# Issuing 32 stores of an inverse transform from ScalarE's DMA queue instead of SyncE's

## The chip, the core and the metric

The kernel runs on one core of a Trainium2 chip. Five engines work side by side, each with its own queue of instructions: TensorE (PE in the profile; its weight loads are shown apart as PEld), VectorE (DVE), ScalarE (ACT), GpSimd (POOL) and SyncE (SP). They wait for each other through semaphores. A DMA is issued by an instruction in the queue of SP, ACT or POOL; the bytes are moved by 16 DMA engines that all queues share, and a counter tells when they have landed. The metric is the device time of one execution in microseconds, lower is better.

## What is computed

The result mixes two branches of the same input `x` (2048 positions, 512 channels) by a gate per position. One branch is a long convolution along the positions, whose taps `K` come from a state-space model and which the reference does by FFT; the other is a dense layer pair with GELU.

```python
x = A_u
g = _sigmoid((x * gate_w).sum(-1, keepdims=True))
P = jnp.exp(logdA[:, :, None] * l[None, None, :])
K = jnp.einsum("dn,dnl,dn->dl", Cc, P, dB).real
Yf = Uf * Kf[None, :, :, :]          # spectra of u and K, padded to 2 L
y = irfft2(Yf, s=(1, L2))[:, :, 0, :L] + u * Dskip
h = _gelu(jnp.einsum("bsd,df->bsf", x, w1) + b1)
b = jnp.einsum("bsf,fd->bsd", h, w2) + b2
return g * a + (1 - g) * b           # a is y
```

## The kernel before

The program has two parts. `front` (to about 420 us of the profile) computes the dense branch, the taps and the first stage of the transforms of taps and signal. A planner with due times sets the order of its instructions; it leaves the first-stage results in DRAM (`tu_d` for the signal, `tk_d` for the taps) and the dense branch's rows in the output. The change does not touch it.

`conv` (L1091 to L1289) does the rest, in an order that is written out by hand. The transform of length 2048 is split into 32 x 64, and `conv` holds the 32 second-stage transforms, two per loop step, so 16 steps `s`. The tiles are 128 partitions x 512 channels of fp32 (256 KB). In step `s`:

- `product(s)` multiplies the spectra of signal and taps on DVE (six operations, L1151 to L1156).
- `signal(s + 1)` runs eight matmuls on PE into the banks `p2u` (L1129), from the tiles `us`, which lie in `den`, `attic` and `loft`.
- `matrices(s // 2 + 1)` in even steps makes the second set of factors `f` from the constants `cc`, by two ACT instructions (L1117, L1118).
- `taps(s + 2)` runs eight matmuls into `p2k` (L1129), four with weights from `cc` and four with weights from `f`, and ACT copies the two banks to `k` (L1137).
- `inverse(s)` runs eight matmuls into the two banks `pa` (L1168).
- `turn(s)` copies each `pa` to one of six buffers `sa` by ACT (L1174) and stores `sa` to the DRAM tensor `t4_d` (L1176; the profile calls it `t_d`). After every eighth row, a group of `t4_d` is complete and is read back in another layout, into `den` and `t3` (profile: `t`), by POOL's queue for the first three groups and by ACT's for the last (L1188).
- In steps 7 to 12 `dense` loads rows of the dense branch from the output by SP's queue (L1202).

At each step's start SP issues the loads that come next: `tk` (L1110), `cc` (L1102), `tu_d` (L1241). So SP's queue holds loads and stores in the order of the loop, and a store that waits for ACT's copy holds back the loads behind it.

After the loop PE does what was left of the dense products (`rest`, L1213 to L1215), and the last transform `pb` over `den` and `t3` (L1273, 64 matmuls); DVE or ACT and POOL apply the gate and add, and the rows go out (L1287, L1289).

Every DMA from SP or ACT also takes one of eight completion counters, DMAHW0 to DMAHW7, in turn, whichever of the two queues issues it. A DMA that takes a counter again first waits until the DMA that carried it last has landed.

Of the kernel before, what the change touches and what calls it, by code (L numbers as in the profile page):

```python
# [275 lines left out]
def gated_mix(  # L276
# [18 lines left out]
    nc = tc.nc  # L295
# [5 lines left out]
    t4_d = dr.tile([4, 2, GROUP, 2, 32, D], F32, name="t4_d")  # L301
# [789 lines left out]
    def conv(pool, ps, late, attic, loft, den):  # L1091


        sas = [pool.tile([P, D], F32, name=f"sa{k}", bufs=1) for k in range(6)]
# [75 lines left out]
        def turn(s):  # L1170

            for n in (2 * s, 2 * s + 1):
                sa = sas[n % 6]
                nc.scalar.copy(sa, pas.pop(n))  # L1174
                g, k = divmod(n, GROUP)
                nc.sync.dma_start(t4_d[g, :, k].rearrange("e c q d -> (c q) e d"), sa)  # L1176
                if k < GROUP - 1:
                    continue
                rows = t4_d[g].rearrange("e k c q d -> (e k c) q d")

                for h in (0, 4, 8, 16, 24) if g == 3 else (0, 8, 16, 24):
                    if h == 24 and g < 2:
                        held.append((t3[g:P:4, 16:24], rows[:, 24:32]))
                        continue
                    on = nc.gpsimd if n < 31 else nc.scalar
                    e = h + (4 if g == 3 and h < 8 else 8)
                    to = t3[g:P:4, h - 8 : e - 8] if h > 7 else den[g:P:4, h:e]
                    on.dma_start(to, rows[:, h:e])  # L1188
# [41 lines left out]
        for s in range(16):  # L1230

            for n in range(2 * s + N_TK + (2 if s else 0), 2 * s + N_TK + 4):
                if n < 24:
                    fetch(n if n < 16 else n + 8)
            if s == 0:
                for n in range(16, 24):
                    fetch(n)
            if s in (2, 4, 6, 8):
                consts(s // 2 + 3)
            for n in range(2 * s + N_ROOM, min(2 * s + N_ROOM + 2, 32)) if s > 3 else ():  # L1240
                nc.sync.dma_start(us[n], tu_d[ko[n]])  # L1241
            product(s)
            if s + 1 < 16:
                signal(s + 1)
            if s + 2 < 16:
                if s % 2 == 0:
                    matrices(s // 2 + 1)
                taps(s + 2)
            if s == 9:
                for to, rows in held:  # L1250
                    nc.gpsimd.dma_start(to, rows)
            if s == 15:
                rest(N_REST)
            inverse(s)
            turn(s)
            if 7 <= s < 13:
                dense(HERE[s - 7], nc.sync)
# [4 lines left out]
        for s in range(4):  # L1262
            m, i = 7 - s // 2, s % 2
            z, g = mos[m][:, i], gate[:, 1, 2 * m + i : 2 * m + i + 1]
            nc.vector.scalar_tensor_tensor(z, accs[s], g, z, ALU.mult, ALU.add)

        for m in range(8):
# [9 lines left out]
            for i in range(2):  # L1277
                t = 2 * m + i
                z, g = mos[m][:, i], gate[:, 0, t : t + 1]
# [90 lines left out]
```

## Time and profile before

| | us |
|---|---|
| median of 3 runs | 530.65 |
| lowest and highest of them | 528.84, 531.64 |
| the profiled execution, its own time | 528.3 |
| its span, first to last instruction | 526.5 |
| PE busy in the span | 509.1 (97%) |
| ACT busy | 353.0 (67%) |
| DVE busy | 428.4 (81%) |
| granted TensorE clock, mean | 0.997 |

A row of the page's list of groups gives the line, the engine and operation, output and inputs by the program's names, the count, and then busy time and the mean of one in ns. A row of the timeline gives start and length in us, the same names, and in brackets how long the engine stood idle before it and what ended that. An engine with a q behind its name is its queue: issuing a DMA or waiting there is not counted as busy. "Landing" is the time from the issue of a DMA until its counter shows that all bytes have arrived. The chain of waits is followed back from the last instruction, at each step to what released it.

### The profile page before, as it was taken

What the parts mean: (1) busy time and instruction counts of PE and PEld (TensorE: products, weight loads), DVE (VectorE), ACT (ScalarE), POOL (GpSimd) and SP (SyncE); (2) the same over time, 40 slices, a digit from 0 to 9 for tenths busy, and PEclk for the clock granted to TensorE, in tenths of its full rate; (3) what the DMA queues carried; (4) which work ended last, traced back from release to release, by engine and by line L of the source; (5) the groups of instructions that cost most, each with busy time, mean ns of one, the idle gap of its engine ahead of it and who ended that gap; (6) DMA issues with size and microseconds to landing.
All of it is one profiled execution on the core that took longest, in us unless ns stands there. A gap on an engine that the chain in (4) does not pass through costs nothing.

```text
span 526.5 us, 12296 instructions
## 1 busy us (share of the span) xinstructions
PE 509.1 (97%) x4858; PEld 387.8 (74%) x4858; DVE 428.4 (81%) x808; ACT 353.0 (67%) x614; POOL 41.6 (8%) x80
## 2 busy tenths in 40 slices
PE   8887999999999999999999999999999999999995
PEld 7656789898889978976988998988988722222551
DVE  6898899999999968879999989999901188777543
ACT  4989946699875689986595998456534545565311
POOL 2000000000000000000012001202010100110123
PEclk9999999999999999999999999999999999999998
DMA  8999664152685434392879026625669899999978
GB/s 241 369 301 285 222 223 153 67 202 54 159 224 201 142 91 132 111 300 86 220 156 301 3 81 126 159 40 121 201 202 172 226 309 319 366 347 375 301 277 329
DMA packets 82517, 107.87 MB, mean 205 GB/s; under 512 B 39334, under 2 KB 43562, under 8 KB 81916
## 3 DMA queue, kind: packets, MB, share of 16 engines
q1 hardware_dynamic: 76476, 85.04, 50.8%
q0 software_dynamic: 5056, 18.65, 14.0%
q10 hardware_dynamic: 928, 3.41, 1.8%
q8 instruction: 38, 0.62, 0.5%
q14 instruction: 19, 0.16, 0.1%
HBM read 61.46 MB, written 45.62 MB: 203 GB/s over the span
## 4 chain that ended last, share of the span: by engine, by line
PE 75%; ACT 11%; DMA 8%; DVE 3%; issue 2%; SPq 1%; ACTq 0%; DVEq 0%
PE pk L693 10%; PE ph L915 8%; PE ph L917 8%; PE ph L916 8%; PE acc L965 8%; PE acc L967 7%; PE acc L966 7%; PE p2u L1129 6%; PE p2k L1129 5%; PE pa L1168 3%; PE pb L1273 3%; DMA tu_d<-attic 2%; PE ph L415 2%; ACT L932 2%; ACT ph L932 2%
## 5 line engine op out<-in xcount | busy, mean ns | idle before, releaser
L915 PE MATMUL ph<-xh,wh 128*128 128x256 f32 x448 | 128.1, 286 | 2.9 <-ACT attic L433 1.8
L917 PE MATMUL ph<-xh,wl 128*128 128x256 f32 x448 | 127.0, 284 | 0.5 <-DVE wl L794 0.4
L916 PE MATMUL ph<-xlo,wh 128*128 128x256 f32 x448 | 126.6, 283 | 0.0
L915 PEld LDWEIGHTS ph<-xh,wh 128*128 128x128 f32 x448 | 85.1, 190 | 11.9 <-issue 5.6
L916 PEld LDWEIGHTS ph<-xlo,wh 128*128 128x128 f32 x448 | 85.2, 190 | 2.0
L917 PEld LDWEIGHTS ph<-xh,wl 128*128 128x128 f32 x448 | 85.1, 190 | 1.2 <-DVE wl L794 1.2
L965 PE MATMUL acc<-wh,hh 128*128 128x512 f32 x206 | 82.9, 403 | 1.3 <-ACT hh L935 1.2
L967 PE MATMUL acc<-wh,hl 128*128 128x512 f32 x206 | 81.1, 394 | 0.4 <-DVE hl L945 0.4
L966 PE MATMUL acc<-wl,hh 128*128 128x512 f32 x206 | 80.9, 393 | 0.0
L932 ACT ACTIVATE ph<-ph,b1t 128x256 f32<-128x256 f32 x112 | 50.4, 450 | 43.3 <-PE ph L917 41.3
L945 DVE TENSOR_TENSOR hl<-ph,hh 128x512 fp32r<-128x512 f32 (+1 forms) x62 | 38.3, 618 | 31.9 <-ACT hh L935 31.6
L693 PE MATMUL pk<-y,den 128*32 128x64 f32 x2048 | 61.4, 290 | 0.0
L693 PEld LDWEIGHTS pk<-y,den 128*32 128x32 f32 x2048 | 57.2, 136 | 3.7 <-issue 1.4
L965 PEld LDWEIGHTS acc<-wh,hh 128*128 128x128 f32 x206 | 38.7, 188 | 15.9 <-issue 6.8
L967 PEld LDWEIGHTS acc<-wh,hl 128*128 128x128 f32 x206 | 38.7, 188 | 10.6 <-DVE hl L945 2.0
L655 DVE TENSOR_TENSOR y<-y,ea 128x64 f32<-128x64 f32 (+4 forms) x80 | 45.2, 566 | 0.2
L966 PEld LDWEIGHTS acc<-wl,hh 128*128 128x128 f32 x206 | 38.7, 188 | 6.5
L935 ACT CAST hh<-ph 128x512 fp32r<-128x512 f32 (+1 forms) x62 | 33.0, 533 | 8.7 <-PE acc L966 5.2
L500 DVE TENSOR_TENSOR loft<-den,zz 128x256 f32<-128x256 f32 (+2 forms) x48 | 37.2, 775 | 1.7 <-ACT den L626 1.3
L501 DVE TENSOR_TENSOR loft<-den,zz 128x256 f32<-128x256 f32 (+2 forms) x48 | 37.1, 773 | 0.0
L668 DVE TENSOR_TENSOR y<-y,loft 128x2048 f32<-128x2048 f32 x16 | 36.5, 2283 | 0.0
L1137 ACT COPY k<-p2k 128x512 f32<-128x512 f32 x32 | 18.8, 586 | 24.9 <-issue 13.1
(183 smaller groups left out, 885.2 us busy)
## 6 DMA issues: line engine op xcount, KB each, us to landing
tu_d<-attic SPq DMA_DIRECT2D x64, 128.0 KB, 3.6
tk_d<-sk SPq DMA_DIRECT2D x32, 256.0 KB, 4.7
t_d<-sa SPq DMA_DIRECT2D x32, 256.0 KB, 6.8
tk<-tk_d SPq DMA_DIRECT2D x24, 256.0 KB, 4.9
t<-t_d POOLq DMA_DIRECT2D x9, 512.0 KB, 8.3
attic<-in_xt_dram SPq DMA_DIRECT2D x16, 256.0 KB, 4.4
xh_d<-xh SPq DMA_DIRECT2D x8, 512.0 KB, 3.2
xl_d<-xlo SPq DMA_DIRECT2D x8, 512.0 KB, 4.9
```

The source lines that it names most:

```text
L500: vec(2 * m, lambda: vv.tensor_mul(t, a, br), due, [ka, *kb], [kt])
L655: nc.vector.tensor_mul(both(n, 64 - 3 * n, n), both(0, 64 - n, n), an)
L693: nc.tensor.matmul(pks[q][32 * j : 32 * j + 32, :, gg], x[:, r, :, ch], y[:, r, :, ch], start=(r == 0), stop=(r == 1), skip_group_check=True,)
L915: nc.tensor.matmul(p, h, xh[xk][:, d], start=(d == 0), stop=False)
L916: nc.tensor.matmul(p, h, xlo[xk][:, d], start=False, stop=False)
L917: nc.tensor.matmul(p, lo, xh[xk][:, d], start=False, stop=(d == 3))
L932: nc.scalar.activation(phs[q][:, n], phs[q][:, n], AF.Gelu_apprx_tanh, bias=b1t[:, f : f + 1])
L945: nc.vector.tensor_sub(lo, phs[q][:, 0:nf], hi.bitcast(F32))
L965: nc.tensor.matmul(a, h, wh[1][w], start=start, stop=False)
L966: nc.tensor.matmul(a, h, wl[1][w], start=False, stop=False)
L967: nc.tensor.matmul(a, l, wh[1][w], start=False, stop=(j == 3))
L1129: nc.tensor.matmul(out[64 * i : 64 * i + 64], w, x, start=True, stop=True)
```

## The change

`turn` now makes both copies of a step first and then issues both stores, from ACT's queue instead of SP's. Everything else is as before; the lines behind L1174 move down by one (L1176 is now L1177, L1188 is L1189, L1202 is L1203).

```diff
             for n in (2 * s, 2 * s + 1):
                 sa = sas[n % 6]
                 nc.scalar.copy(sa, pas.pop(n))
+            for n in (2 * s, 2 * s + 1):
                 g, k = divmod(n, GROUP)
-                nc.sync.dma_start(t4_d[g, :, k].rearrange("e c q d -> (c q) e d"), sa)
+                nc.scalar.dma_start(t4_d[g, :, k].rearrange("e c q d -> (c q) e d"), sas[n % 6])
                 if k < GROUP - 1:
                     continue
```

ACT's queue where step 1 ends and step 2 begins (`sa_4794` and `sa_4795` are the two buffers of step 1, `f_4967` the factors that `taps(4)` needs in step 2; the brackets name what an instruction waits for):

```order
 L1174 COPY sa_4794<-pa_4937 128x512 [waits PE_49]
 L1174 COPY sa_4795<-pa_4940 128x512 [waits PE_49]
+L1177 DMA t_d<-sa_4794 64x2x512 [waits DMAHW2_49,Activation_49]
+L1177 DMA t_d<-sa_4795 64x2x512 [waits DMAHW3_49,Activation_49]
 L1117 ACTIVATE f_4967<-cc_4814 64x256 [waits DMAHW0_49]
 L1118 COPY f_4967<-cc_4814 64x256
```

The two stores now stand between the copies of `pa` and the two instructions that make `f`. The second waits for the counter DMAHW3, which the second store of step 0 carried last.

ACT's queue in the change, from the stores of step 4 to the factors of step 6 (`sa_4794` and `sa_4795` are again the buffers of step 4, `sa_4796` and `sa_4797` those of step 5):

```order
L1177 DMA t_d<-sa_4794 64x2x512 [waits DMAHW2_49,Activation_49]
L1177 DMA t_d<-sa_4795 64x2x512 [waits DMAHW4_49,Activation_49]
L1137 COPY k_5099<-p2k_5096 128x512 [waits DVE_49,PE_49]
L1137 COPY k_5104<-p2k_5101 128x512 [waits PE_49]
L1174 COPY sa_4796<-pa_5106 128x512 [waits DMAHW6_49,PE_49]
L1174 COPY sa_4797<-pa_5109 128x512 [waits DMAHW7_49,PE_49]
L1177 DMA t_d<-sa_4796 64x2x512 [waits DMAHW0_49,Activation_49]
L1177 DMA t_d<-sa_4797 64x2x512 [waits DMAHW2_49,Activation_49]
L1117 ACTIVATE f_5137<-cc_4951 64x256 [waits DMAHW1_49]
L1118 COPY f_5137<-cc_4951 64x256
```

The first store of step 4 takes DMAHW2, and the second of step 5 is the next to take it, one step later.

SP's queue from step 6 on, as the difference:

```order
+L1242 DMA attic<-tu_d 128x512
+L1203 DMA attic<-out_dram 128x2x512
 L1102 DMA cc_5198<-in_c_dram 128x384
-L1176 DMA t_d<-sa_4796 64x2x512
-L1176 DMA t_d<-sa_4797 64x2x512
-L1202 DMA attic<-out_dram 128x2x512
-L1176 DMA t_d<-sa_4792 64x2x512
-L1176 DMA t_d<-sa_4793 64x2x512
-L1202 DMA attic<-out_dram 128x2x512
```

SP keeps the loads alone, and the loads of the dense rows no longer stand behind stores.

## The prediction, made before the changed kernel ran

> **What bounds the kernel now.** I read the page's chain first, then the window table of the last stage (the one the change touches), then the chain in order of time, then the timeline of one loop step.
>
> ```profile
> PE 75%; ACT 11%; DMA 8%; DVE 3%; issue 2%; SPq 1%; ACTq 0%; DVEq 0%
> ```
>
> ```profile
> 424.50:491.90 67.40, 67.40 (x355) 18.49 (x351) 54.76 (x90) 37.76 (x71) 6.20 (x12) 1.00 0.95 334
> 491.90:505.60 13.70, 13.70 (x62) 10.09 (x62) 4.17 (x7) 2.15 (x4) 0.00 (x0) 1.00 0.80 273
> 505.60:520.10 14.50, 13.96 (x65) 5.34 (x64) 7.59 (x11) 4.12 (x6) 7.38 (x6) 1.00 0.99 368
> 520.10:526.50 6.40, 0.00 (x0) 0.00 (x0) 0.67 (x1) 0.00 (x0) 0.23 (x1) 0.72 0.66 254
> ```
>
> The columns are stretch, sum, busy time of PE, PEld, DVE, ACT and POOL, granted clock, DMA share, GB/s. In the loop (first row) PE is busy all 67.40 us at clock 1.00; ACT is busy 37.76 of them and the DMA engines 0.95. So TensorE sets the loop's length, ACT has 44% to spare, and the DMA engines are nearly full. PE goes on without a gap to 505.6.
>
> ```profile
> 433.74 1.87 PE p2u L1129 x8
> 435.61 1.72 PE p2k L1129 x8
> 437.32 1.02 PE pa L1168 x8
> 438.34 1.87 PE p2u L1129 x8
> 496.51 6.42 DMA t_d<-sa
> 503.02 2.87 DMA den<-t_d
> 506.02 13.97 PE pb L1273 x64
> 520.02 0.75 DVE attic L1285
> ```
>
> A step lasts 438.34 - 433.74 = 4.60 us and is three PE pieces. SP's stores (L1176) appear on the chain only once: the last one lands 6.42 us after its issue at 496.51. Even there PE has the leftover dense products until 505.6, so what that landing costs is the gap up to 506.02, 0.42 us.
>
> **What the change can gain.** It cannot shorten the 67.40 us that are all PE. Two places are left. The first is the 0.42 us gap. The second is the tail after 520.1, which waits for output stores behind DMA engines that are 0.99 busy from 505.6 on. In the row before, 20% of 13.70 us = 2.7 us of DMA time is idle, because loads wait for the last t4_d stores; stores that land sooner could use at most that, so the tail is worth 0 to 2.7 us. Output stores are still released one pair at a time by PE's products and the last by DVE at 520.8. I take the gap in full and 0.4 us of the tail: **-0.8 us**, between 0 and -3.1.
>
> **What it costs: ACT's own queue.** This is an even step before:
>
> ```profile
> 433.80 1.07 ACT L1174 COPY sa<-pa 128x512 f32<-128x512 f32 x2 [0.37 <-PE pa L1168]
> 434.41 1.18 SPq L1176 DMA_DIRECT2D t_d<-sa  x2
> 434.90 0.41 ACT L1117 ACTIVATE f<-cc 64x256 f32<-64x256 f32 x1
> 435.32 0.40 ACT L1118 COPY f<-cc 64x256 f32<-64x256 f32 x1
> 435.87 0.14 PEld L1129 LDWEIGHTS p2k<-tk,f 128*64 128x64 f32 x2 [0.28 <-ACT f L1118]
> 436.30 1.03 PE L1129 MATMUL p2k<-tk,f 128*64 128x512 f32 x4
> 436.58 0.59 ACT L1137 COPY k<-p2k 128x512 f32<-128x512 f32 x1 [0.86 <-ACT f L1118]
> ```
>
> Right behind the two evictions sa stand the two copies that build f (L1117, L1118), and PE multiplies by f in the same step at 436.30. The stores now stand between them. The copies occur six times behind stores:
>
> ```profile
> L1117 ACT ACTIVATE f<-cc x6: 414/414/415, 434.9 to 480.9; 64x256 f32<-64x256 f32 x6
> L1176 SPq DMA_DIRECT2D t_d<-sa x32: 518/544/1326, 429.8 to 496.5; - x32
> 503.02 1.16 ACTq L1188 DMA_DIRECT2D den<-t_d  x2
> 504.28 1.84 ACTq L1188 DMA_DIRECT2D t<-t_d  x3
> ```
>
> An issue takes 0.544 us on SP (up to 1.326), and on ACT's queue 1.16 / 2 = 0.58 to 1.84 / 3 = 0.61 us. How late may f be? The start of the stage shows PE waiting for it:
>
> ```profile
> 419.72 0.40 ACT L1118 COPY f<-cc 64x256 f32<-64x256 f32 x1
> 420.17 1.08 PE L1129 MATMUL p2k<-tk,f 128*64 128x512 f32 x4 [0.80 <-ACT f L1118]
> L1137 ACTq EVENT_SEMAPHORE  x1: 2673/2673/2673, 433.9 to 433.9; - x1
> ```
>
> PE starts 0.05 us after f ends (420.12 to 420.17). In the step above f ends at 435.72 and is wanted by 436.30 - 0.05 = 436.25: a slack of 0.53 us. From below: the first store starts while the second eviction still runs, as SP's did (434.41, when the first eviction was done), the pair takes SP's 1.18 us to 435.59, f runs 435.62 to 436.44, PE starts at 436.49: 0.2 us late. From above: ACT issues only when both evictions are done (434.87) and takes 2 x 0.61 us, f runs 436.11 to 436.93, PE starts 0.7 us late; with issues as long as SP's slowest, nearly 1 us, f would run 436.90 to 437.72 and PE be 1.5 us late. The last row speaks for the lower end: ACT's queue stood at the wait of the k copy (L1137) at 433.9, 0.1 us after the first eviction began, with three instructions still to run; the queue goes ahead of its engine, so a store can be issued beside an eviction. Issues in a stage with a DMA share of 0.95 are sometimes long, though. I take 0.35 us a step: 6 x 0.35 = **+2.1 us**, between 1.2 and 6 (a mean of 1 us a step).
>
> The Trainium skill, Perfetto Trace Analysis, section on per-engine timelines, says that ACT's compute instructions are pushed into a wait queue and the sequencer goes on, while a DMA holds the sequencer until its descriptors are written. The trace agrees for the first half (the row at 433.9); by that rule alone the term would be 6 x 0.2 = 1.2 us and the sum below 0.9 us less.
>
> Odd steps have no f:
>
> ```profile
> 429.20 1.07 ACT L1174 COPY sa<-pa 128x512 f32<-128x512 f32 x2 [0.36 <-PE pa L1168]
> 431.98 0.59 ACT L1137 COPY k<-p2k 128x512 f32<-128x512 f32 x1 [1.71 <-issue]
> ```
>
> ACT idles 1.71 us between them and the pair of issues fits, so those cost nothing. If that cover were gone, k would be late, and it is read by DVE two steps on. SP is rid of 32 x 0.544 = 17.4 us of issuing that bounded nothing; its loads (tk, cc, the dense rows) come forward, and as PE had no gap, none was late.
>
> **Waits that ACT takes over.** The order shows each DMA waiting for one of eight counters (DMAHW0 to 7) used in turn: it may start only when the DMA that last carried its counter has landed. SP paid this before:
>
> ```profile
> SPq L1110 <- DMA t_d<-sa: 2.6, 2, 2.4
> 447.47 0.54 POOL L1188 DMA_DIRECT2D den<-t_d  x1 [33.50 <-DVE v L1155]
> 448.07 1.05 POOL L1188 DMA_DIRECT2D t<-t_d  x2
> 452.83 1.69 SPq L1176 DMA_DIRECT2D t_d<-sa  x2
> ```
>
> A tk load that reads nothing of t4_d waited up to 2.4 us for a store. Nobody felt it, since only loads stood behind. Now such a wait stands on ACT in front of f. In the order of the change the second store of step 1 waits for the second of step 0, 4.6 us older (DMAHW3), and the second of step 5 for the first of step 4 (DMAHW2). How long stores take to land, from issues of SP in three places:
>
> ```profile
> L1176 SPq DMA_DIRECT2D t_d<-sa x2: 552/562/572, 429.8 to 430.5; - x2
> DMA to landing us min/median/max: 6.8/6.8/6.8
> ...
> L1176 SPq DMA_DIRECT2D t_d<-sa x2: 530/542/553, 443.6 to 444.2; - x2
> DMA to landing us min/median/max: 2.4/2.4/2.4
> ...
> L1176 SPq DMA_DIRECT2D t_d<-sa x2: 530/554/579, 448.2 to 448.9; - x2
> DMA to landing us min/median/max: 8.7/8.7/8.7
> ```
>
> With 6.8 us the store of step 0 lands at 430.5 + 6.8 = 437.3 where step 1 wants to go on at 435.0: 2.3 us. With 8.7 us that of step 4 lands at 448.2 + 8.7 = 456.9, where step 5 wants to issue its second store 0.6 us after the 452.83 of its first: 3.5 us. Together 5.8 us from above. From below nothing: with 2.4 us both are in time. In a queue of its own a store no longer stands behind eight t loads (step 0), but at 448 POOL's three 512 KB loads take the engines whichever queue the store is in. I take nothing for step 1 and about half of 3.5 for step 5: **+1.8 us**.
>
> **Sum.** 2.1 + 1.8 - 0.8 = +3.1 us on a profiled execution of 528.3 us (span 526.5): 531.4. That execution is 2.3 us under the median of the runs shown, 530.65, on which the forecast is 530.65 + 3.1 = 533.8 us, 0.6% slower. I call a difference under 0.5% (2.65 us) no change, since that is about what a measurement of this kernel can tell; the three runs alone spread by 2.8 us.
>
> The Trainium skill, DMA: Bandwidth & Descriptors, section "Issuing engines are not separate DMA queues", says that issuing from several engines saves only the sequencer's issue time. Without the 0.4 us of tail that I granted to the separate queue the sum would be +3.5 us; no run here shows it yet.
>
> **Rivals.**
>
> *ACT issues only behind its own evictions, and slowly.* For it: issues of SP up to 1.326 us, DMA share 0.95. Against: the queue's place at 433.9. 6 x 1.0 + 1.8 - 0.8 = +7.0 us: 537.7.
>
> *Hidden after all.* The issues overlap the evictions, the stores land at 2.4 to 5 us in their own queue, and no counter is waited for: 1.2 + 0 - 1.5 (half of the 3.1 us at the end) = -0.3 us: 530.4, no change. For it: ACT's 44% of spare time, 0.53 us of slack. Against: the copies of f stand directly behind the stores, and the burst at 448.
>
> *Faster: the last stores.* One mechanism: today the last store needs 6.42 us because SP's queue is full ahead of it; alone in a queue it lands in 2.4 us, the loads for the final products come 4 us sooner, and the idle 2.7 us of DMA time before 505.6 is filled, so the output finds free engines. Price -0.42 - 2.7 = -3.1 us with the f copies costing nothing: 527.5. It decides only if f is late by less than 0.1 us a step. Against it: POOL's loads are in flight then too, and f has to end 0.53 us after where it ends now while 1.2 us are put ahead of it.
>
> The Trainium skill, Perfetto Trace Analysis, section DMA Optimizations, advises giving inputs to one issuing engine and outputs to another. By that rule this last rival would win.
>
> **How the numbers follow.** Forecast 0.50 (its own range 532 to 536), slow issue 0.22, hidden 0.23, faster 0.05. A quarter of the forecast's weight lies under +2.65 us. Slower: 0.50 x 0.75 + 0.22 = 0.6; within 0.5%: 0.125 + 0.23 = 0.35; faster 0.05. The range runs from 529.5 (hidden, less a run's spread) to 539 (slow issue with a little of the counters' upper bound).
>
> **What would show it.** f's first copy some 0.7 us later behind sa (1.8 instead of 1.1 us) in six steps; idle time of PE before p2k<-tk,f, released by ACT f, of about 0.35 us each; one longer gap around 453 to 456 where an ACT store waits for a landing; odd steps still 4.60 us long; PE's pb starting without the 0.42 us gap. I am wrong if even steps stay at 4.60 us (then f had more slack than I read), if odd steps stretch, or if PE waits for tk or attic loads.

## The result, and the profile after

With the stores on ScalarE's queue the kernel takes 532.81 us (median of 22 runs, 530.25 to 538.04), the kernel before, in the same measurement, 528.54 us (22 runs). The ratio is 1.0081 with a 95% interval of 1.0060 to 1.0102: 0.8% slower, 4.3 us by the medians, 3.2 to 5.4 us by the interval. The forecast was +3.1 us. The kernel before had a median 2.1 us lower here than in the three runs that the forecast was added to, so the difference, not the 533.8, is what the forecast has to be measured by. The profiled execution took 531.52 us, its span 529.7. Three executions in the measurements below, one each of three kernels, ran at a granted clock of 0.56 and took about 790 us; every median and ratio here leaves them out.

The chain of waits by engine, in the page of the changed kernel:

```profile
PE 73%; ACT 11%; DMA 7%; DVE 4%; issue 3%; SPq 1%; ACTq 1%; DVEq 0%
```

PE loses two points, and ACTq, the queue of ACT, has 1% where it had 0.

The window table of the changed kernel, cut at the same events as before: the loop, the leftover products, `pb`, the end.

```profile
424.50:496.55 72.05, 68.66 (x355) 17.92 (x351) 54.69 (x90) 37.53 (x71) 6.18 (x12) 1.00 0.93 325
496.55:510.20 13.65, 13.65 (x63) 10.11 (x63) 4.19 (x7) 2.15 (x4) 0.00 (x0) 1.00 0.81 282
510.20:524.25 14.05, 13.95 (x65) 4.51 (x64) 7.56 (x11) 4.12 (x6) 7.38 (x6) 1.00 0.87 326
524.25:529.70 5.45, 0.00 (x0) 0.00 (x0) 0.70 (x1) 0.00 (x0) 0.27 (x1) 0.91 0.67 251
```

The loop is 4.65 us longer for the same 355 matmuls at the same clock of 1.00, and TensorE, busy all of the stretch before, now idles 72.05 - 68.66 = 3.39 us of it. The other stretches are as long as before or shorter.

The chain in order of time shows what stands there instead. This is step 4 of the changed kernel, a step with nothing unusual in it (start, length, engine, output, line):

```profile
443.50 1.06 PE pa L1168 x8
...
445.06 0.60 ACT sa L1174
...
445.81 0.56 ACTq L1177
...
446.84 0.41 ACT f L1118
...
447.30 1.07 PE p2k L1129 x3
```

Before, a step was three PE pieces in a row. Now the chain leaves PE after `pa`, goes through ACT's second eviction (until 445.66), the issue of the second store (445.81 to 446.37), the copies of `f`, and comes back to PE at 447.30.

The timeline of ACT, for steps 2, 4, 6 and 8 of the changed kernel (L1174 are the two evictions, L1177 the two stores together; in brackets what ended the idle time):

```profile
433.76 1.07 ACT L1174 COPY sa<-pa 128x512 f32<-128x512 f32 x2 [0.42 <-PE pa L1168]
434.37 2.51 ACTq L1177 DMA_DIRECT2D t_d<-sa  x2
436.93 0.41 ACT L1117 ACTIVATE f<-cc 64x256 f32<-64x256 f32 x1 [2.10 <-DMA t_d<-sa]
...
444.57 1.07 ACT L1174 COPY sa<-pa 128x512 f32<-128x512 f32 x2 [0.42 <-PE pa L1168]
445.19 1.18 ACTq L1177 DMA_DIRECT2D t_d<-sa  x2
446.42 0.41 ACT L1117 ACTIVATE f<-cc 64x256 f32<-64x256 f32 x1 [0.77 <-ACT sa L1174]
...
454.67 2.01 ACTq L1177 DMA_DIRECT2D t_d<-sa  x2
456.73 0.41 ACT L1117 ACTIVATE f<-cc 64x256 f32<-64x256 f32 x1 [1.60 <-issue]
...
465.34 1.58 ACTq L1177 DMA_DIRECT2D t_d<-sa  x2
466.96 0.41 ACT L1117 ACTIVATE f<-cc 64x256 f32<-64x256 f32 x1 [1.42 <-DMA attic<-tu_d]
```

A pair of stores takes 1.18 us where nothing holds it (step 4), in the other three 2.51, 2.01 and 1.58. In steps 2 and 8 the second store waited for a DMA to land, in step 6 its issue alone was long.

How much each step lost can't be read from PE's idle time alone. From the timeline of PE I took the start of the first matmul into `pa` in every step and the distance to that of the step before; the "loop" is from step 0 to step 15. All odd steps up to 13 are 4.60 us in both kernels.

| us | loop | step 2 | 4 | 6 | 8 | 10 | 12 |
|---|---|---|---|---|---|---|---|
| before | 66.05 | 4.60 | 4.60 | 4.60 | 4.60 | 4.60 | 4.60 |
| changed | 70.73 | 6.21 | 4.88 | 5.71 | 5.63 | 4.99 | 4.91 |
| changed, profiled again | 71.74 | 7.88 | 4.88 | 5.00 | 5.63 | 4.90 | 5.02 |

The loop's 4.7 to 5.7 us account for the 4.3 us of the medians. In steps 2, 4 and 6 of the first profile a simple sum gives the loss: a step loses what `f` ends later behind the start of the evictions than it did before (1.92 us), less the slack of 0.53 us, plus 0.05 us because the first matmuls after a wait take 1.08 us in place of 1.03. For step 2: `f` starts at 436.93, its second copy ends at 437.76, 4.00 us behind 433.76; 4.00 - 1.92 - 0.53 + 0.05 = 1.60, measured 1.61. (In step 8 the evictions start late as well, held up by the stores of step 6.)

### The profile page after: what moved, and what is told of

Read it like the earlier page. It is cut to its first block, busy times and chain, and to the rows that moved or that the text cites. A ratio compares the mean times of both kernels' runs of the same rounds, so it can differ in the third digit from the quotient of the medians.

```text
span 529.7 us, 12267 instructions
## 1 busy us (share of the span) xinstructions
PE 512.7 (97%) x4858; PEld 389.3 (73%) x4858; DVE 428.5 (81%) x808; ACT 352.5 (67%) x614; POOL 41.6 (8%) x80
## 4 chain that ended last, share of the span: by engine, by line
PE 73%; ACT 11%; DMA 7%; DVE 4%; issue 3%; SPq 1%; ACTq 1%; DVEq 0%
PE pk L693 9%; PE ph L915 8%; PE ph L917 8%; PE ph L916 8%; PE acc L965 8%; PE acc L967 7%; PE acc L966 7%; PE p2k L1129 4%; PE p2u L1129 4%; PE pa L1168 3%; PE pb L1274 3%; PE ph L415 2%; DMA tu_d<-attic 2%; ACT L932 1%; DMA xh_d<-xh 1%
```

## The experiments

Two theories stand behind them. **The place:** what costs is that two DMA issues stand in ACT's queue ahead of `f`, with all that a store there may wait for. **The DMA side:** what costs is the traffic itself, stores that land at other times in a queue of their own. Ratios are to the kernel before, run beside each on the same chip.

**f one step earlier.** Against the changed kernel: the stores stay on ACT; the two copies of `f` move ahead of them into the odd step before.

```diff
-                if s % 2 == 0:
-                    matrices(s // 2 + 1)
+                if s == 0:
+                    matrices(1)
                 taps(s + 2)
+                if s % 2 and s + 3 < 16:
+                    matrices(s // 2 + 2)
```

> The stores stay with ACT, but the two copies that build f are made in the odd step before, behind the copies of k, so that no store stands ahead of them. Theory A (the loss comes only from f behind the stores: about 0.3 us of issuing in each of six even steps plus waits for counters, 4.7 us in the profile, and the tail gains 1.5): PE runs the loop without a gap again, pa of step 15 starts at about 494 us instead of 498.8, and the time ends 1 to 1.5 us below before (ratio 0.997 to 0.998). Rival B (two queues disturb each other at the DMA engines, loads come late): still 1.006 to 1.010. Rival C (ACT simply has 32 x 0.56 = 18 us more to do): still 1.006 to 1.010.

Measured: 528.82 us, ratio 1.0002 (0.9981 to 1.0024); all steps 4.60, loop 66.04. The timeline of ACT in this kernel, where step 2 begins:

```profile
434.67 0.40 ACT L1118 COPY f<-cc 64x256 f32<-64x256 f32 x1
435.09 1.07 ACT L1174 COPY sa<-pa 128x512 f32<-128x512 f32 x2
435.71 3.76 ACTq L1177 DMA_DIRECT2D t_d<-sa  x2
439.56 1.07 ACT L1137 COPY k<-p2k 128x512 f32<-128x512 f32 x2 [3.40 <-DVE v L1156]
```

The pair of stores held ACT's queue for 3.76 us, longer than in the profile above, and PE lost nothing, because `f` was already there and only the copies of `k` came late. So the same stores in the same queue cost nothing once `f` does not stand behind them. The gain at the end that was expected on top did not come.

**Both copies first, stores on SP.** The other half of the diff alone, against the kernel before.

```diff
                 nc.scalar.copy(sa, pas.pop(n))
+            for n in (2 * s, 2 * s + 1):
                 g, k = divmod(n, GROUP)
-                nc.sync.dma_start(t4_d[g, :, k].rearrange("e c q d -> (c q) e d"), sa)
+                nc.sync.dma_start(t4_d[g, :, k].rearrange("e c q d -> (c q) e d"), sas[n % 6])
```

> Only the other half of the change: both copies of a step first, then both stores, but from SP as before. Theories A, B and C: same as before, 0.998 to 1.002. A rival by which the new order of copies and stores itself costs something: up to 1.008.

Measured: 528.28 us, ratio 0.9998 (0.9974 to 1.0023), loop as before. The new order of copies and stores is free.

**Half of the stores.** Two kernels, one with the stores of even steps on ACT and one with those of odd steps (the two queues exchanged), the rest on SP.

```diff
-                nc.scalar.dma_start(t4_d[g, :, k].rearrange("e c q d -> (c q) e d"), sas[n % 6])
+                (nc.sync if s % 2 else nc.scalar).dma_start(t4_d[g, :, k].rearrange("e c q d -> (c q) e d"), sas[n % 6])
```

> ACT issues the 16 stores of the even steps (an odd step, without f, follows each); SP issues the others. Theory A: the issues fall into the 1.7 us that ACT idles before k, counters may hold ACT up to 1.5 us without PE noticing; loop as before, time 0.997 to 1.002. Rival C: half the loss, +2.1 us, 1.004. Rival B: between 1.002 and 1.008.

> ACT issues the 16 stores of the odd steps, of which twelve stand ahead of f; SP issues the others. Theory A: six gaps of PE before p2k<-tk,f of at least 0.3 us each, 1.9 us, plus 0 to 3 us of counter waits, less up to 1 us at the tail: +1.5 to +4.5 us, 1.003 to 1.008, and clearly above the run with the even steps. Rival C: +2.1 us, the same as the even steps.

Measured, even: 528.87 us, ratio 1.0010 (0.9986 to 1.0034), loop 66.40; only step 8 is longer, 4.96. Odd: 533.56 us, ratio 1.0091 (1.0060 to 1.0123), a little over the 1.008 expected, loop 69.42; steps 2 to 12: 5.80, 4.91, 4.96, 5.56, 4.88, 4.88. The stores of odd steps are the ones that stand ahead of `f`, and they alone carry the loss; an equal share for both halves falls. The 0.36 us of the even half is a spill: the pair of step 6 took 2.06 us in ACT's queue, and the odd step 7 could not make all of it up.

**f late without any DMA.** Against the kernel before: the stores stay on SP, and the two copies of `f` are made twice.

```diff
-            nc.scalar.mul(f1[0:64], f[64:128], -1.0)
-            nc.scalar.copy(f1[64:128], f[0:64])
+            for _ in range(2 if m > 1 else 1):
+                nc.scalar.mul(f1[0:64], f[64:128], -1.0)
+                nc.scalar.copy(f1[64:128], f[0:64])
```

> The stores stay in SP's queue; the two copies that make f are made twice over (the same values), so f is ready 0.41 + 0.40 = 0.81 us later in each of the six even steps and no DMA stands on ACT. Theory A (what costs is the place in ACT's queue ahead of f): 0.81 - 0.53 of slack = 0.28 us in each of the six steps, all alike, odd steps 4.60: the loop from the first pa to the last grows by 1.7 us to 67.7, ratio about 1.003. Rival D (the loss comes from the DMA side: stores that land at other times, a queue that is shared otherwise): the loop stays at 66.0 us, ratio 1.000.

Measured: 531.13 us, ratio 1.0044 (1.0026 to 1.0062), loop 68.50. All six even steps are alike, 5.02, and the loop's 2.46 us more are 0.41 for each. The timeline of PE in this kernel:

```profile
437.38 1.08 PE L1130 MATMUL p2k<-tk,f 128*64 128x512 f32 x4 [0.19 <-ACT f L1119]
...
447.00 1.08 PE L1130 MATMUL p2k<-tk,f 128*64 128x512 f32 x4 [0.19 <-ACT f L1119]
```

Making `f` late by itself slows the kernel, with every DMA where it was: the place theory holds, the DMA side falls as the cause of this part. 0.28 us a step was expected and 0.41 came: the first copy starts 1.09 us behind the evictions as before, but four copies one behind the other end 0.88 us later and not 0.81, and 0.05 us go for the restart of the matmuls. The idle time in the brackets is 0.19 us for a step that is 0.41 longer, so of each wait some 0.2 us are counted as busy; the length of the step is the figure to read.

**Four issues a step.** Each store split in two of 128 KB.

```diff
-                nc.scalar.dma_start(t4_d[g, :, k].rearrange("e c q d -> (c q) e d"), sas[n % 6])
+                for h in range(2):
+                    nc.scalar.dma_start(t4_d[g, :, k, h].rearrange("e q d -> q e d"), sas[n % 6][64 * h : 64 * h + 64])
```

> The change with each store split in two of 128 KB, so that ACT issues four in a step, 64 in all, the same bytes. Theory A: two more issues of 0.53 to 0.6 us ahead of f in each even step, so the clean even steps are 1.1 to 1.2 us longer than with the change (about 6.0 us in place of 4.9), and the counters come round sooner: loop +7 to +15 us over 66.0, ratio 1.013 to 1.03. Odd steps have 1.71 us of idle ACT for 2.3 us of issues and may grow by up to 0.6. Rival D (bytes and landings count, not issues): as the change, loop 70 to 71, ratio 1.008.

Measured: 553.13 us, ratio 1.0450 (1.0413 to 1.0488), loop 92.30. The even steps with issues alone, 4, 8 and 10, are 6.49, 6.29 and 6.25, 1.3 to 1.6 us over the 4.93 that the clean steps of the change take on the mean. Steps 2, 6 and 12 are 9.76, 12.65 and 7.75, and odd steps grow too (6.27, 6.62 and 5.63 in steps 3, 7 and 13). ACT and PE of this kernel at step 2, two timelines:

```profile
438.93 2.50 ACTq L1178 DMA_DIRECT2D t_d<-sa  x4
441.47 0.41 ACT L1117 ACTIVATE f<-cc 64x256 f32<-64x256 f32 x1 [3.99 <-DMA tk<-tk_d]
```

```profile
442.35 1.12 PE L1129 MATMUL p2k<-tk,f 128*64 128x512 f32 x2 [4.04 <-ACT f L1118]
```

Issues are what counts, not bytes, as the place theory says; but 26 us of loop lie far beyond its 7 to 15. The expectation had counted the issues (about 1.2 us in six steps) and undersized the waits. The clean steps lose 1.65 to 1.88 us against before, so six steps of issues are about 10 us; the other 16 us come with the waits, since twice as many stores bring the eight counters round sooner, and with what a late ACT hands on to the next steps. The 3.99 us in the row above are not one wait, and the `tk` load that the row names did not cause it: by the counters in the trace the first of the four stores waited until 438.9 for a load of taps into `t`, issued at 432.7, and the four issues then took 2.50 us. In step 6 a store waited 5.25 us, until 470.2, for the counter of one of ACT's own stores, issued at 460.7. How the 16 us divide between waits and delays handed on stays open.

**Fewer loads that take counters.** The change, with the `tk` loads merged in pairs.

```diff
+            if n % 2:
+                return
...
-            nc.sync.dma_start(t2s[n], tk_d[ko[n]])
+            nc.sync.dma_start(two, tk_d[ko[n] : ko[n] + 9 : 8].rearrange("k p d -> p k d"))
```

> The change, with the tk loads of SP merged into pairs (512 KB in one DMA, half as many DMAs), so that a counter comes round about a third later and is less often still taken. Theory C (what the even steps lose beyond 0.3 us is waits for counters of loads that have not landed): steps 2 and 8 lose 1.0 to 2.0 us less together, the clean steps keep their 0.3 us: loop 67.9 to 69.5 us in place of 70.7, ratio 1.002 to 1.006. Rival E (the extra loss is the issue itself, long when the DMA engines are full): the loop stays at 70 to 71, ratio 1.008. If PE waits for the merged loads, steps stretch in other places and the run says nothing on C.

Measured: 532.22 us, ratio 1.0061 (1.0039 to 1.0083), loop 69.32; steps 2 to 12: 5.13, 4.88, 5.07, 5.65, 4.98, 5.20. ACT's timeline in this kernel, steps 2 and 8:

```profile
434.68 1.42 ACTq L1180 DMA_DIRECT2D t_d<-sa  x2
436.14 0.42 ACT L1120 ACTIVATE f<-cc 64x256 f32<-64x256 f32 x1 [1.01 <-issue]
...
465.56 0.41 ACT L1120 ACTIVATE f<-cc 64x256 f32<-64x256 f32 x1 [1.54 <-DMA attic<-tu_d]
```

Step 2 has lost its wait for a landing, and 1.1 us with it. Step 8 is the same to 0.02 us: it waits for a load of `tu_d`, which the edit did not touch. So the wait follows the counter, in the one step where the edit moved it; the issue part stays. (In step 2 of the change a store carried that counter, not a load as the expectation has it.) The loop falls into the expected range, but the times do not tell this kernel from the change: its interval overlaps that of the change, 1.0060 to 1.0102.

**Another queue altogether.** The 32 stores from POOL's queue.

```diff
-                nc.scalar.dma_start(t4_d[g, :, k].rearrange("e c q d -> (c q) e d"), sas[n % 6])
+                nc.gpsimd.dma_start(t4_d[g, :, k].rearrange("e c q d -> (c q) e d"), sas[n % 6])
```

> The same 32 stores, both copies first, issued by POOL's queue in place of ACT's; POOL is busy 6.2 us in the loop and nothing of PE's stands behind it, and its DMAs take none of the eight counters that SP and ACT share. Theory A: every step 4.60, loop 66.0 us, ratio 0.998 to 1.002. Rival D (any separate queue for the stores disturbs the loads): loop longer by over 1 us. A store behind POOL's reads of the groups lands late, and the last one may delay pb by 0 to 3 us.

Measured: 531.43 us, ratio 1.0056 (1.0037 to 1.0076), outside what the place theory expected. The loop is 66.55, with only step 8 longer (5.14); that is 0.5 us over the place theory and under the 1 us of rival D. In this kernel ACT's timeline at step 8 and POOL's near the end of the loop read:

```profile
462.55 0.59 ACT L1174 COPY sa<-pa 128x512 f32<-128x512 f32 x1 [0.70 <-DMA t_d<-sa]
463.73 0.59 ACT L1174 COPY sa<-pa 128x512 f32<-128x512 f32 x1 [0.59 <-DMA t_d<-sa]
```

```profile
492.47 3.05 POOL L1177 DMA_DIRECT2D t_d<-sa  x5
496.12 0.61 POOL L1177 DMA_DIRECT2D t_d<-sa  x1 [0.60 <-DMA t<-t_d]
501.03 1.24 POOL L1177 DMA_DIRECT2D t_d<-sa  x2 [4.29 <-ACT sa L1174]
```

POOL's queue holds the reads of the groups as well, and stores wait behind them: five go out together at 492.47, ACT waits for a free `sa`, and `pb` starts with a gap of 0.81 us. Loop and gap make 1.3 of the 3.0 us. The kernel was profiled again for the rest.

> The POOL version profiled a second time, to see where its 3.0 us over before lie, of which the loop (0.5) and the gap ahead of pb (0.8) explain 1.3. Theory G (the last stores leave POOL late and the tail is later for it, so it belongs to the kernel): gap 0.6 to 1.0 us and 8 us or more from the end of pb to the end again. Rival T0 (the end varies by execution): gap 0.5 to 1.0, end 6.1 to 7.5 us, and 1.7 us stay without a place.

Measured: loop 66.15, no gap, and from the start of the last matmul of `pb` (the expectations call it the end of `pb`) to the end of the span 8.54 us, after 8.47 the first time. The gap does not belong to the kernel. The long end repeated, but a kernel with SP's stores, the one with `f` made twice, had 8.73, so I leave open why POOL's version is 3 us slower.

**The change again.** The same kernel, a second profile.

> The changed kernel as it is, profiled a second time, to see which pieces of the loss repeat. Theory A and C: the issue part repeats to 0.1 us (steps 4, 10 and 12: 4.88 to 5.0 us); the waits for counters of loads stand in the same places, steps 2 and 8, each 0.3 to 1.5 us over the clean step, because order and counters are fixed; step 6, whose second issue took 1.39 us with no wait on a counter, need not repeat and falls to 4.9 to 5.2 if it was chance. Loop 69.5 to 71.0 us. Rival F (the extra is chance contention of one execution): the long steps sit elsewhere, or the loop is under 69.

Measured: one time of 533.38 us, loop 71.74, a little over the range; the steps stand in the table above. Steps 2 and 8 are long again, and step 6 falls to 5.00: its 1.39 us issue did not come again. ACT's timeline at steps 2 and 6 of this second profile:

```profile
435.37 4.05 ACTq L1177 DMA_DIRECT2D t_d<-sa  x2
439.46 0.41 ACT L1117 ACTIVATE f<-cc 64x256 f32<-64x256 f32 x1 [3.77 <-DMA tk<-tk_d]
...
457.21 1.30 ACTq L1177 DMA_DIRECT2D t_d<-sa  x2
458.55 0.41 ACT L1117 ACTIVATE f<-cc 64x256 f32<-64x256 f32 x1 [0.89 <-ACT sa L1174]
```

The row of step 2 names a `tk` load, but the releaser in the brackets is inferred. By the order of the change the second store waits for the counter DMAHW3, which the second store of step 0 carried, as in the first profile. These are the two stores of step 0 in the second profile, with the landing of the second:

```profile
L1177 ACTq DMA_DIRECT2D t_d<-sa x2: 544/589/634, 430.6 to 431.4; - x2
...
DMA to landing us min/median/max: 7.4/7.4/7.4
```

Issued at 431.4, it landed at 438.8, and the store that waited for it went out at 438.89. The place of the wait in step 2 is fixed, its length is not: 3.28 us of loss here, twice the 1.61 of the first profile and beyond the 1.5 us over a clean step that were expected. The long waits in steps 2 and 8 are not chance contention of one execution.

**Only the last four stores.** Those of steps 14 and 15 on ACT, where no `f` follows.

```diff
-                nc.scalar.dma_start(t4_d[g, :, k].rearrange("e c q d -> (c q) e d"), sas[n % 6])
+                (nc.sync if s < 14 else nc.scalar).dma_start(t4_d[g, :, k].rearrange("e c q d -> (c q) e d"), sas[n % 6])
```

> The stores of steps 14 and 15 alone are issued by ACT, the 28 others by SP as before. No f stands behind these four. Theory T0 (no gain at the end: TensorE has the leftover products until about 505.6 and the output stores wait for its products): loop 66.0 us, ratio 0.999 to 1.001. Theory T1 (the tail of the prediction): the 0.42 us gap goes and up to 2.7 us of the tail, ratio 0.994 to 0.9985.

Measured: 528.41 us, ratio 1.0005 (0.9985 to 1.0026), loop 66.04. Nothing is gained; a gain of more than 0.15%, 0.8 us, is excluded.

**The kernel before again.**

> The kernel before, profiled a second time, to see whether the 0.42 us gap ahead of pb and the 7.1 us from the end of pb to the end of the span belong to it. Theory T0 (both vary from execution to execution): the gap may be 0 and the end 6.1 to 8.8 us. Theory T1 (both come from the stores in SP's queue): gap 0.3 to 0.6 us, end 6.9 to 7.3. The loop is 66.0 us either way.

Measured: loop 66.04, and 7.66 us from the last matmul of `pb` to the end. Its chain has no gap ahead of `pb`:

```profile
506.48 0.23 PE acc L1215
506.70 13.91 PE pb L1273 x64
```

So the 0.42 us gap, on which a term of the forecast stood, was a property of one execution.

## Why the prediction was right, and where it was not

**The bound and the sign: right.** PE set the loop's length, the stores of SP cost it nothing, and `f` behind two issues is late. The run with `f` made early (ratio 1.0002) and the run with `f` made late without a DMA (1.0044) show both halves of it.

**The issue term, +2.1 us: right.** 0.35 us in six steps was forecast. The steps in which nothing waited, 4, 10 and 12, lost 0.28, 0.39 and 0.31 us in the first profile and 0.28, 0.30 and 0.42 in the second: 0.33 on the mean, 2.0 us for six. `f` starts 1.85 us behind the evictions in step 4, where 1.8 was forecast. The sum from below had the mechanism: the first store goes out at 445.19, while the second eviction still runs, and only the second issue is exposed. It gave 0.2 us; `f` ended 0.75 us later, which is 0.22 us over the slack, and 0.05 us of restart, which I had not thought of, make the 0.28.

In the first row of step 2 above, the first store is issued at 434.37, while the evictions run until 434.83. The Trainium skill, Perfetto Trace Analysis, section Per-engine timelines, has compute instructions of ACT waiting in a queue of their own while the sequencer goes on; the trace agrees, and the issue term by that rule alone, 1.2 us, came within 0.8 us of the measured one.

**The counter term, +1.8 us: the mechanism right, the places wrong, the size near in one profile by luck.** What the loop lost beyond the issues was 4.7 - 2.0 = 2.7 us in the first profile, 0.8 of it the long issue in step 6 and 1.9 waits, and 5.7 - 2.0 = 3.7 us in the second. That 1.9 lies so near to 1.8 is luck: none of the 1.8 us came where the prediction had put it. It chose between ends for two waits:

- *Nothing for the second store of step 1*, where it had written 2.3 us as the upper end. That is the step that failed. The reason given was that in its own queue a store no longer stands behind eight `t` loads. These are landings in the changed kernel, of the second store of step 0 and then of the first of step 4:

```profile
L1177 ACTq DMA_DIRECT2D t_d<-sa x1: 551/551/551, 430.5 to 430.5; - x1
...
DMA to landing us min/median/max: 5.8/5.8/5.8
...
L1177 ACTq DMA_DIRECT2D t_d<-sa x1: 526/526/526, 450.1 to 450.1; - x1
...
DMA to landing us min/median/max: 4.8/4.8/4.8
```

  Issued at 430.5, it landed at 436.3, and the store that waited for its counter went out at 436.36. It cost 1.3 us over a clean step in the first profile and 3.0 in the second. On ACT this landing took 5.8 and 7.4 us in the two profiles of the change and 7.5 in the kernel with `f` made early; on SP it took 6.8 and 7.2 us in the two profiles of the kernel before. So a queue of its own brought nothing that these profiles show: the loads of SP share the same DMA engines. The Trainium skill, DMA: Bandwidth & Descriptors, section "Issuing engines are not separate DMA queues", says that all issuers' DMAs interleave on the same 16 engines; these landings agree.

- *Half of 3.5 us for the second store of step 5.* Nothing came. The 8.7 us of landing were those of a store that met POOL's three loads at 447.5; after the change the store of step 4 was issued at 450.1 and POOL's loads came at 453.1, so it landed after 4.8 us, before its counter was asked for again.

- *Step 8*, which the prediction did not have: 1.03 us in both profiles. The second store of step 7 waits for the counter of a `tu_d` load that SP issued at 454.5 and that landed at 466.3 (first profile). From 456 to 459 POOL's loads were 0.74 of the 1.02 MB that the DMA engines moved. The second store of step 6 had been held too, until 462.8, by the counter of a `tk` load issued at 453.0, which made the evictions late. The prediction looked for stores that wait for stores; the counters are shared with SP's loads too, and those were long in this stretch.

**The tail, -0.8 us: not shown.** Its first half, the gap of 0.42 us, was absent in the kernel before when it was profiled again. For the second, the span from the start of the last matmul of `pb` on was 7.14 and 7.66 us before and 6.18 both times with the change, with the output stores landing faster, first in the kernel before and then in the changed one (DMA issues after 505 us, median landing last):

```profile
out_dram<-attic SPq DMA_DIRECT2D x3, 512.0 KB, 4.3
```

```profile
out_dram<-attic SPq DMA_DIRECT2D x3, 512.0 KB, 2.8
```

The kernel with both copies first and SP's stores has 3.2 us there and 6.17 for the end, with a loop of the old length, and the one with `f` made twice has 8.73. The end varies by 2.6 us among kernels that keep the stores on SP, and with all stores on ACT it is not always short: 6.91 with `f` made early and 6.97 with the `tk` loads merged. So the change can't be given credit for its 6.18. It may still have gained up to about a microsecond: the loop lost 4.7 and 5.7 us, the medians differ by 4.3. That stays open. The Trainium skill, Perfetto Trace Analysis, section DMA Optimizations, advises one issuing engine for inputs and another for outputs; with 1.0002 for the kernel in which that separation costs PE nothing, no run here shows a gain from it.

**The sum.** 2.1 + 1.8 - 0.8 = 3.1 against 4.3: the issues were sized well, the waits for counters were put into the wrong steps and 0.1 to 1.9 us too low, a long issue of 0.8 us came in one profile, and no run shows the tail. Of the rivals, the hidden case falls with step 4 at 4.88. Slow issue had the right neighbourhood in the total, but not the mechanism: steps with issues alone lost 0.33 us and not 1.0. Its upper bound also reads SP's slowest issue as nearly 1 us where the prediction's own row has 1.326; the long one of step 6 took 1.39.

**What was to show it.** Odd steps of 4.60 us and no wait of PE for `tk` or `attic` held. The long gap at 453 to 456 was there (0.89 us of idle PE at 457.61) and would have passed for a confirmation, but it was a long issue and not a counter, and the second profile does not have it.

## What to carry to other kernels

Price a DMA issue on a compute engine by what stands behind it in that queue and how much slack that has, not by the engine's spare time: ACT was idle 44% of the loop and the stores still cost 0.8%, and with the two copies moved ahead of them no loss was measured (1.0002). Where queues share completion counters, an issue can wait for another queue's load, so write down for each issue whose landing it waits for, and do not put that wait at nothing when the DMA engines are nearly full: of the two waits priced here one cost 1.3 and 3.0 us, the other nothing, and a third was not on the list. Before a gap or a tail in one profile is put into a sum, ask for a second execution: here 0.42 us of gap went by itself, and the end differed by 2.6 us among kernels that keep the stores where they were.

## What was not expected of the hardware

- A wait whose place is fixed by order and counters changed its length by 1.7 us between two executions of one kernel (step 2, 6.21 and 7.88 us), more than the whole difference between step 2 and a clean step in the first of them.
- Doubling the issues of one queue did not double the loss but took it from 4.7 to 26 us of loop: about 10 us by the steps with issues alone, and 16 us more with the waits for landings.
- The profile shows 0.19 us of idle PE for a step that is 0.41 us longer.
